# Retention in front of two feed-forward layers: late tokens in 64-token steps of all heads and two batches

## The chip, the cores and the metric

The kernel runs on one core of a Trainium2 chip. The metric is the device time of one execution in microseconds (us). TensorE multiplies matrices (rows named PE; PEld is the loading of its stationary operand), VectorE is DVE, ScalarE is ACT, GpSimd is POOL, and SyncE (SP) issues most of the DMAs. TensorE writes into PSUM, eight banks of 512 float columns in each of 128 partitions.

## The reference

Three layers follow each other: a retention with a decay for each head, and two feed-forward layers over all 3072 tokens.

```python
# q, k, v: (batch 4, heads 8, tokens 768, 64)
for t in range(768):
    state = gamma * state + outer(k[t], v[t])    # per batch and head, 64 x 64
    y[t]  = scale * q[t] @ state                 # gamma = 1 - 2**(-5 - head)
x  = y as (3072 tokens, 512)
x  = ELU(x @ w_in) @ w_out                       # 512 -> 2048 -> 512
h  = x @ w_in2
out = (P(h) / Q(h)) @ w_out2                     # P cubic, Q quadratic in |h|
```

## The kernel before

**Two phases.** Phase 0 is the retention and the first feed-forward layer, phase 1 the second one. The tokens go in six tiles `j` of 512 columns (`x_t[j]`), the hidden layer in 16 slices `f` of 128. One iteration of the loop in phase 0 is a pair (j, f). Its order is written out by hand in `seq`: tile 0 with f 0 to 7 (iterations 0 to 7), all of tile 1 (8 to 23), tile 0 with f 8 to 15 (24 to 31), then tiles 2, 3, 4 and 5 (32 to 95).

**One iteration.** `g1(h, f, ...)` is 12 matmuls into one PSUM bank `h`: each operand is split into a high part and a rest, and three products are summed. ACT makes Relu (L580) and Exp (L581), DVE joins them (L585), ACT rounds the result to `gh` (L593), POOL makes the rest `gl` (L594; on DVE in iterations 0 to 23). `g2` of the iteration before (`pend`) is 12 matmuls into four accumulators: eight that need `gh`, then four that need `gl`. So h of an iteration has a whole g2 and the next g1 on TensorE to be turned into gh and gl. After the last slice of a tile, `evac` copies the accumulators and stores them. The weights of both layers come as 64-bit floats and are narrowed and split by ACT, DVE and POOL beside this (`narrow`, `split_w`; iterations 0 to 18, and with odd f in tiles 2 to 4).

**Retention.** Each batch is cut into six chunks of 128 tokens, 24 chunks in all, batch after batch. A visit (an item i) does four heads of one chunk, so there are 48. Items 0 to 7 stand ahead of the loop, 8 to 15 in iterations 0 to 7, 16 to 23 in iterations 24 to 31, 24 to 47 in the iterations with even f of tiles 2 to 4. In a visit `at_out(i)` multiplies the state by q (not in a batch's first chunk), the masked scores by v, and the keys by v for the new state (not in its last), and `at_in(i + 1)` makes the next visit's scores q k. All these are plain float matmuls of 64 x 64 quarters of TensorE, with 64 or 128 columns; the four quarters are given in turn. The trace counts two passes for each such matmul: a visit's 28 matmuls are 56 rows. DVE masks the scores (L255), ACT and DVE make the high part and the rest of the output in the x tile (L320, L321), and write the new state. The visit stands between g1 and g2 on TensorE.

From chunk 8 on (the four batches' later chunks), the diagonal half-blocks of scores are laid out so that the output and the state come in two sums, and ACT and DVE add them (L316, L317, L307, L309); POOL scales q and k by the decay (L213, L216). The first eight chunks (`NV = 8`) keep the state's decay on TensorE by a diagonal matrix (`diag`), have their keys and queries scaled on DVE (L213, L216, called by `scale_chunk`), and the state's matmuls use two of the four quarters only.

**PSUM.** Four banks are accumulators, two are `h` (`psh`), two the tile of the visits (`T_t`). **DMA.** `load_chunk` fetches a chunk's q, k, v in three transfers of 512, 512 and 256 KB; SP's queue issues them and the weights in program order.

Of the kernel before, what the change touches and what calls it, by code (L numbers as in the profile page):

```python
# [21 lines left out]
C = 128  # L22
NP = H // 2
# [27 lines left out]
def decay_tables():  # L51

    g = 1.0 - 2.0 ** (-5.0 - np.arange(H, dtype=np.float64))
    scale = 1.0 / np.sqrt(D)
    t = np.arange(C)
    lag = np.maximum(t[None, :] - t[:, None], 0)
    full = scale * g[:, None, None] ** lag * (t[None, :] >= t[:, None])
    mask = np.zeros((2, 128, 2, 2, 3 * D))
    for q in range(2):
        for e in range(2):  # L60
            m0, m1 = full[4 * q + e], full[4 * q + 2 + e]
            mask[0, :D, q, e] = np.concatenate([m0[:D], m0[D:, D:]], axis=1)
# [8 lines left out]
    gc = rows(g ** C)  # L71
    gq = rows(scale * g[:, None] ** (t[None, :] + 1.0))
    dg = (gc[:, :, None] * np.tile(np.eye(D), (2, 1))[:, None, :]).reshape(128, -1)
    tab = np.concatenate([mask[0].reshape(128, -1), own_half(gk[None, :, :, None]).reshape(128, -1), gq, dg,
                          mask[1].reshape(128, -1), turned_halves(gk, 0), gc], axis=1)
    return np.ascontiguousarray(tab, dtype=np.float32)


@with_exitstack
def retention_ffn_kernel(ctx: ExitStack, tc: tile.TileContext, qkv, w1i, w1o, w2i, w2o, a_, b_, tab, out):  # L80
# [3 lines left out]
    CB = S // C  # L84
# [14 lines left out]
    atw = at.enter_context(tc.tile_pool(name="atw", bufs=2))  # L99
    psh = at.enter_context(tc.tile_pool(name="psh", bufs=2, space=PSUM))  # L100
    pst = at.enter_context(tc.tile_pool(name="pst", bufs=1, space=PSUM))
    NI = NCH * 2
# [61 lines left out]
    tab_t = acon.tile([128, 1292], F32, name="tab_t")  # L164
    gq_t = tab_t[:, 0:512].rearrange("p (g e t) -> p g e t", g=2, e=2)
    mk = [None, tab_t[:, 512:1288]]
    gc_t = tab_t[:, 1288:1292].rearrange("p (g e) -> p g e", g=2)
    St = acon.tile([128, 2, 2, D], F32, name="St")
    su = acon.tile([128, 2, D], F32, name="su")
# [17 lines left out]
    def of(c):  # L187
        qk, vk, q1 = pieces(c % 4 if c < 8 else c % 2)
# [4 lines left out]

    def load_qk(c):
        nc.sync.dma_start(out=pieces(c % 4 if c < 8 else c % 2)[0], in_=qkv[c, :, 0:1024])

    def load_rest(c):
        qk, vk, q1 = pieces(c % 4 if c < 8 else c % 2)
# [10 lines left out]

    def scale_chunk(c):  # L210
# [7 lines left out]
    A_t = {}  # L218
# [13 lines left out]
    def at_in(i):  # L232

        if i >= NI:
            return
        c, g = divmod(i, 2)
        q2, k2 = of(c)[0:2]
        T = T_t[i]
        if c < NV:
            for n in range(2):  # L240
                for p, e in ((0, 0), (0, 1), (1, 0), (1, 1)):
                    mm(T[R[p], e, 128 * n:128 + 64 * n], k2[R[e], 2 * g + p, D * n:D * n + D],
                       q2[R[e], 2 * g + p, D * n:C])
            return
        for p, e in ((0, 0), (0, 1), (1, 0), (1, 1)):
            mm(T[R[p], e, 64 * p:64 * p + 128], k2[R[e], 2 * g + p, 0:D], q2[R[e], 2 * g + p, :])
        for p, e in ((0, 0), (0, 1), (1, 0), (1, 1)):
            mm(T[R[1 - p], e, 128 * p:128 * p + D], k2[R[e], 2 * g + p, D:C], q2[R[e], 2 * g + p, D:C])

    def at_mask(i):  # L250
        if i >= NI:
            return
        A = atw.tile([128, 2, 192], F32, tag="A", name="A")
        A_t[i] = A
        nc.vector.tensor_tensor(out=A, in0=T_t[i][:, :, 0:192], in1=mk[i >= 2 * NV][:, 384 * (i % 2):384 * (i % 2) + 384]  # L255
                                .rearrange("p (e t) -> p e t", e=2), op=ALU.mult)

    def at_out(i):
# [3 lines left out]
        A, T = A_t.pop(i), T_t[i]  # L262
        four = ((0, 0), (1, 0), (0, 1), (1, 1))
        if c % CB:
            for p, e in four:
                mm(T[R[e], p, 192:320], St[R[p], g, e, :], q1[R[p], g, e, :], stop=False)
        if c < NV:
            at = lambda x, p, e, n: x[R[p], 4 * g + 2 * e + n, :]
            for n in range(2):
                for p, e in four:  # L270
                    mm(T[R[e], p, 192 + D * n:320], at(v, p, e, n), A[R[p], e, 128 * n:128 + 64 * n],
                       start=c % CB == 0 and n == 0, stop=n == 1)
            if c % CB != CB - 1:
                for e in range(2):
                    if c % CB:
                        for p in range(2):
                            mm(T[R[p], p, 384 + D * e:448 + D * e], diag[R[p], g, e, :], St[R[p], g, e, :], stop=False)
                    for n in range(2):
                        for p in range(2):
                            mm(T[R[p], p, 384 + D * e:448 + D * e], at(kn, p, e, n), at(v, p, e, n),  # L280
                               start=c % CB == 0 and n == 0, stop=n == 1)
            return
        for p, e in four:
            mm(T[R[e], p, 192:320], v[R[p], 4 * g + 2 * p + e, :], A[R[p], e, 64 * p:64 * p + 128], start=c % CB == 0)
        for p, e in four:
            mm(T[R[e], 1 - p, 320:384], v[R[1 - p], 4 * g + 2 * p + e, :], A[R[1 - p], e, 128 * p:128 * p + D])
        if c % CB != CB - 1:
            for e in range(2):
                for r, p in four:
                    h = 4 * g + 2 * p + e  # L290
                    mm(T[R[p], r, 384 + D * e:384 + D * e + D], kn[R[r], h, :], v[R[r], h, :])

    def at_state(i):
        c, g = divmod(i, 2)
        T, S = T_t[i], St[:, g]
        a, b = (T[:, r, 384:512].rearrange("p (e d) -> p e d", e=2) for r in range(2))
        if c % CB == CB - 1:
            return
        if c < NV:
            for p in range(2):  # L300
                nc.scalar.copy(S[R[p]], T[R[p], p, 384:512].rearrange("p (e d) -> p e d", e=2))  # L301
            return
        if c % CB == 0:
            nc.vector.tensor_copy(S, a)
        else:
            for e in range(2):
                nc.vector.scalar_tensor_tensor(out=S[:, e], in0=S[:, e], scalar=gc_t[:, g, e:e + 1], in1=a[:, e],  # L307
                                               op0=ALU.mult, op1=ALU.add)
        nc.vector.tensor_tensor(out=S, in0=S, in1=b, op=ALU.add)  # L309

    def at_x(i):
        c, g = divmod(i, 2)
        T = T_t[i]
        if c >= NV:
            for p in range(2):
                nc.scalar.copy(su[:, p], T[:, 1 - p, 320:384])  # L316
            nc.vector.tensor_tensor(out=T[:, :, 256:320], in0=T[:, :, 256:320], in1=su, op=ALU.add)  # L317
        o = T[:, :, 192:320]
        xs = [x[:, 2 * g:2 * g + 2, c % 4 * C:c % 4 * C + C] for x in x_tile(c // 4)]
        nc.scalar.copy(xs[0], o)  # L320
        return lambda: nc.vector.tensor_tensor(out=xs[1], in0=o, in1=xs[0].bitcast(F32), op=ALU.subtract)  # L321

# [14 lines left out]
    def g2(ph, j, f, gh, gl):  # L337
# [3 lines left out]
        if first:  # L341
            acc[ph, j] = [psa.tile([128, 512], F32, tag=f"acc{m}", name=f"acc{m}") for m in range(4)]
        ps = acc[ph, j]
        if ph == 1 and j == NB - 1 and f == KF - 1:
            for m in range(4):
# [3 lines left out]
                t0 = j * 512 + m * 128  # L349
# [10 lines left out]
        for lo in range(2):  # L360
# [7 lines left out]
        if last:  # L368
# [10 lines left out]
    def evac(ph, j, f):  # L379
        ps = acc.pop((ph, j))  # L380
        sign = -1.0 if ph else 1.0
        for a in range(2):
# [17 lines left out]
            else:  # L400
                t0 = j * 512 + a * 256
# [28 lines left out]
    mk[0] = t0[:, 0:776]  # L430
    diag = late("i13")[:, 0:256].rearrange("p (g e d) -> p g e d", g=2, e=2)
    load_qk(0)
    nc.scalar.dma_start(out=mk[0], in_=tab[:, 0:776])
# [3 lines left out]
    nc.scalar.dma_start(out=tab_t[:, 0:512], in_=tab[:, 776:1288])  # L437
    nc.scalar.dma_start(out=diag.rearrange("p g e d -> p (g e d)"), in_=tab[:, 1288:1544])
# [61 lines left out]
    for i in range(UP + 1, NI):  # L500
        T_t[i] = tiles[0]
# [240 lines left out]
```

## Time and profile before

| | |
|---|---|
| median of three runs | 1147.39 us (1147.37 to 1148.6) |
| the profiled execution | 1147.05 us, its span 1144.9 us |
| TensorE busy | 1127.5 us, 98% of the span |
| VectorE, ScalarE, GpSimd busy | 738.6, 702.5, 373.9 us |
| chain that ended last | TensorE 95% of the span |
| HBM | 79.84 MB read, 22.02 MB written |

The span is the stretch between the first and the last instruction in the profile; 2.15 us of the profiled execution lie outside it. Busy TensorE isn't TensorE at its peak, but where its work follows without a gap, its rows give the price of each piece of work.

### The profile page before, as it was taken

The numbers are of one execution on the slowest core, as the hardware profiler recorded it, in microseconds if no ns is written. First come the engines' busy times: TensorE is split into PE (matmuls) and PEld (weight loads), VectorE is DVE, ScalarE is ACT, GpSimd is POOL, SyncE is SP. The second block draws the span as 40 slices with busy tenths as digits, with TensorE's granted clock in tenths as the row PEclk, the third lists the DMA queues.
The fourth block names the chain that finished last, engine by engine and source line by source line (L and its number), as shares of the span: only waits on it lengthen the run. The fifth ranks groups of instructions, "written<-read, shape, count | busy, mean of one in ns | idle before, by whom it ended". The sixth has DMA issues, their size and how long they took to land.

```text
span 1144.9 us, 18306 instructions
## 1 busy us (share of the span) xinstructions
PE 1127.5 (98%) x7196; PEld 926.7 (81%) x7196; DVE 738.6 (65%) x1133; ACT 702.5 (61%) x1246; POOL 373.9 (33%) x289
## 2 busy tenths in 40 slices
PE   7799999999999999999999999999999999999998
PEld 6578888788888888888888888888888888888887
DVE  4887733354454454444353988888887888887875
ACT  3788733344444444445677877777767776776765
POOL 0334212333232243223786323322332232232222
PEclk9999999999999999999999999999999999999999
DMA  8666303263324434313554000200200200200000
GB/s 314 230 220 226 119 13 102 75 212 126 105 77 162 138 105 170 107 56 120 195 190 139 20 1 1 74 1 1 74 1 1 73 1 1 74 1 1 37 1 37
DMA packets 38229, 103.03 MB, mean 90 GB/s; under 512 B 4352, under 2 KB 4480, under 8 KB 38144
## 3 DMA queue, kind: packets, MB, share of 16 engines
q1 hardware_dynamic: 37280, 100.82, 26.4%
q8 instruction: 56, 0.92, 0.3%
q10 hardware_dynamic: 864, 1.06, 0.3%
q14 instruction: 29, 0.24, 0.1%
HBM read 79.84 MB, written 22.02 MB: 89 GB/s over the span
## 4 chain that ended last, share of the span: by engine, by line
PE 95%; ACT 1%; DVE 1%; POOL 1%; DMA 1%; issue 0%; SPq 0%; DVEq 0%; ACTq 0%; POOLq 0%
PE acc L325 46%; PE h L325 45%; PE r L230 5%; DMA ch<-in_qkv_dram 1%; DMA st<-in_w1o_dram 0%; POOL ch L216 0%; DVE A L255 0%; POOL gl L594 0%; POOL ch L213 0%; DVE ch L213 0%; ACT st L134 0%; ACT St L301 0%; ACT wc L132 0%; ACT xh L320 0%; POOL wo L160 0%
## 5 line engine op out<-in xcount | busy, mean ns | idle before, releaser
L325 PE MATMUL h<-xh,wi 128*128 128x512 f32 x1536 | 504.8, 390 | 4.2 <-POOL wi L160 3.0
L325 PEld LDWEIGHTS h<-xh,wi 128*128 128x128 f32 x1536 | 287.9, 188 | 66.9 <-POOL wi L160 5.6
L325 PE MATMUL h<-xl,wi 128*128 128x512 f32 x768 | 298.9, 389 | 0.0
L670 POOL TENSOR_TENSOR gl<-e,gh 128x512 fp32r<-128x512 f32 x96 | 124.8, 1300 | 349.5 <-ACT gh L669 213.3
L325 PE MATMUL acc<-gh,wo 128*128 128x512 f32 x768 | 195.2, 396 | 0.0
L325 PE MATMUL acc<-wo,gh 128*128 128x512 f32 x768 | 190.1, 389 | 0.0
L594 POOL TENSOR_TENSOR gl<-t,gh 128x512 fp32r<-128x512 f32 x72 | 94.1, 1307 | 293.2 <-ACT gh L593 191.8
L585 DVE SCALAR_TENSOR_TENSOR t<-t,h 128x512 f32<-128x512 f32 x72 | 49.5, 687 | 200.2 <-ACT t L581 200.2
L325 PEld LDWEIGHTS acc<-wo,gh 128*128 128x128 f32 x768 | 144.1, 188 | 29.9
L325 PEld LDWEIGHTS h<-xl,wi 128*128 128x128 f32 x768 | 144.1, 188 | 29.9
L325 PEld LDWEIGHTS acc<-gh,wo 128*128 128x128 f32 x768 | 141.1, 188 | 30.7
L580 ACT ACTIVATE t<-h 128x512 f32<-128x512 f32 x96 | 57.4, 598 | 159.4 <-PE h L325 145.2
L644 ACT ACTIVATE s<-h 128x512 f32<-128x512 f32 x96 | 57.4, 598 | 137.0 <-PE h L325 137.0
L650 DVE SCALAR_TENSOR_TENSOR u<-s,b,u 128x512 f32<-128x512 f32 x96 | 72.0, 750 | 55.8 <-ACT u L645 55.3
L325 PE MATMUL acc<-wo,gl 128*128 128x512 f32 x384 | 103.1, 389 | 0.0
L325 PE MATMUL acc<-gl,wo 128*128 128x512 f32 x384 | 102.9, 390 | 0.0
L660 DVE SCALAR_TENSOR_TENSOR e<-e,ab,r 128x512 f32<-128x512 f32 x96 | 72.2, 752 | 32.1 <-ACT r L654 32.1
L661 DVE SCALAR_TENSOR_TENSOR u<-u,r 128x512 f32<-128x512 f32 x96 | 87.7, 914 | 0.0
L325 PEld LDWEIGHTS acc<-gl,wo 128*128 128x128 f32 x384 | 72.1, 188 | 15.5
L325 PEld LDWEIGHTS acc<-wo,gl 128*128 128x128 f32 x384 | 72.0, 188 | 14.9
L646 ACT ACTIVATE e<-h,ab 128x512 f32<-128x512 f32 x96 | 75.4, 785 | 0.0
L653 DVE SCALAR_TENSOR_TENSOR e<-e,ab,h 128x512 f32<-128x512 f32 x96 | 71.8, 748 | 3.4
(83 smaller groups left out, 1338.4 us busy)
## 6 DMA issues: line engine op xcount, KB each, us to landing
ch<-in_qkv_dram SPq DMA_DIRECT2D x36, 512.0 KB, 4.8
st<-in_w1i_dram SPq DMA_DIRECT2D x16, 512.0 KB, 3.7
st<-in_w1o_dram SPq DMA_DIRECT2D x16, 512.0 KB, 4.6
st<-in_w2i_dram SPq DMA_DIRECT2D x16, 512.0 KB, 3.8
st<-in_w2o_dram SPq DMA_DIRECT2D x16, 512.0 KB, 4.6
wc<-w2s SPq DMA_DIRECT2D x32, 256.0 KB, 2.9
w2s<-wc SPq DMA_DIRECT2D x24, 256.0 KB, 2.2
xs<-y SPq DMA_DIRECT2D x24, 256.0 KB, 3.9
```

Of the source, the lines that this page charges most:

```text
L230: nc.tensor.matmul(out=out, lhsT=lhsT, rhs=rhs, start=start, stop=stop)
L325: nc.tensor.matmul(out=ps, lhsT=lh, rhs=rh, start=first and idx == 0, stop=last and idx == len(pairs) - 1)
L580: nc.scalar.activation(out=t, in_=h, func=ACTF.Relu, scale=-1.0)
L585: nc.vector.scalar_tensor_tensor(out=y, in0=t, scalar=-1.0, in1=h, op0=ALU.add, op1=ALU.max)
L594: (nc.vector if early else nc.gpsimd).tensor_tensor(out=gl, in0=y, in1=gh.bitcast(F32), op=ALU.subtract)
L644: nc.scalar.activation(out=s, in_=ps, func=ACTF.Square)
L646: nc.scalar.activation(out=e, in_=ps, func=ACTF.Identity, scale=ab[:, 3:4], bias=ab[:, 2:3])
L650: nc.vector.scalar_tensor_tensor(out=u, in0=s, scalar=b1, in1=u, op0=ALU.mult, op1=ALU.add)
L653: nc.vector.scalar_tensor_tensor(out=e, in0=e, scalar=ab[:, 1:2], in1=ps, op0=ALU.add, op1=ALU.mult)
L660: nc.vector.scalar_tensor_tensor(out=e, in0=e, scalar=ab[:, 0:1], in1=r, op0=ALU.add, op1=ALU.mult)
L661: nc.vector.scalar_tensor_tensor(out=u, in0=u, scalar=QC, in1=r, op0=ALU.add, op1=ALU.mult)
L670: nc.gpsimd.tensor_tensor(out=gl, in0=e, in1=gh.bitcast(F32), op=ALU.subtract)
```

## The change

The first eight chunks are now tokens 0 to 511 of batches 0 and 1, taken in turn (chunk c is batch c % 2), so the first two have no state before them, and all eight hand one on. All later tokens go in 64-token steps. A step takes all eight heads of two batches at once, in two halves s (one batch each). There are 16: steps 8 to 11 are the rest of batches 0 and 1 (iterations 25, 27, 29, 31), steps 12 to 23 batches 2 and 3 (f 1, 5, 9, 13 of tiles 2 to 4). Step 11 and 23 hand no state on, step 12 has none before it. In a step TensorE does g2 of the iteration before, then for each half the output and the state (`st_out`) and the next step's scores (`st_in`), then the eight gh matmuls of its own g2; the four gl matmuls follow the next iteration's g1. The output is scaled by decay on DVE after the matmuls (`st_y`) instead of q before them; ACT makes the decayed state (`st_decay`) for DVE to add (`st_sum`); POOL scales the keys alone, an iteration later. After iteration 23 the two h banks and the visits' tile become two tiles `V_t` of two banks: h of odd f is a bank of `V_t[1]`, of even f of `V_t[0]`, and the steps use columns of all four. Each x tile now holds 256 tokens of two batches, and `row` finds their place in the output.

```diff
+L = 64
...
-    CB = S // C
+    CB = S // L
...
     def load_rest(c):
-        qk, vk, q1 = pieces(c % 4 if c < 8 else c % 2)
-        if c % CB == CB - 1:
-            nc.sync.dma_start(out=vk[:, 0:512], in_=qkv[c, :, 1024:1536])
-        else:
-            nc.sync.dma_start(out=vk, in_=qkv[c, :, 1024:2048])
-        if c % CB:
+        qk, vk, q1 = pieces(c % 4)
+        nc.sync.dma_start(out=vk, in_=qkv[c, :, 1024:2048])
+        if c >= 2:
             nc.sync.dma_start(out=q1, in_=qkv[c, :, 2048:2560])
+    def load_step(n):
+        qk, vk, vq = pieces(n % 2)
+        nc.sync.dma_start(out=qk, in_=qkv[n, :, 0:1024])
...
     def scale_chunk(c):
         q2, k2, v, kn, q1 = of(c)
-        if c % CB:
-            (nc.vector if c < NV else nc.gpsimd).tensor_tensor(out=q1, in0=q1, in1=gq_t, op=ALU.mult)
-        if c % CB != CB - 1:
-            gk = mk[c >= NV][:, 768:776]
-            (nc.vector if 2 <= c < NV else nc.gpsimd).tensor_tensor(out=kn, in0=kn, in1=gk.to_broadcast([128, H, D]), op=ALU.mult)
+        if c >= 2:
+            nc.vector.tensor_tensor(out=q1, in0=q1, in1=gq_t, op=ALU.mult)
+        gk = mk[:, 768:776]
+        (nc.vector if c >= 2 else nc.gpsimd).tensor_tensor(out=kn, in0=kn, in1=gk.to_broadcast([128, H, D]), op=ALU.mult)
+
+    def scale_keys(n):
+        if n < NCH and n % CB != CB - 1:
+            kn = of_step(n)[3].rearrange("p b z s t -> p (b z) (s t)")
+            nc.gpsimd.tensor_tensor(out=kn, in0=kn, in1=gk_t.to_broadcast([128, 4, 2 * D]), op=ALU.mult)
...
+    four = ((0, 0), (1, 1), (0, 1), (1, 0))
+    def st_in(n, s):
+        if n >= NCH:
+            return
+        q2, k2 = of_step(n)[0:2]
+        T = U_t[n][s]
+        for z in range(2):
+            for a, r in four:
+                mm(T[R[r], a, z, 0:64], k2[R[a], r, z, s, :], q2[R[a], r, z, s, :])
+    def st_mask(n, s):
...
+        nc.vector.tensor_tensor(out=A, in0=U_t[n][s][:, :, :, 0:64], in1=mk_t, op=ALU.mult)
+    def st_out(n, s):
...
+        for z in range(2):
+            if n % CB:
+                for r, a in four:
+                    mm(T[R[a], r, 128 + 64 * z:192 + 64 * z], St[R[r], a, z, s, :],
+                       q2[R[r], r, z, s, :] if a == r else qf[R[r], z, s, :], stop=False)
+            for r, a in four:
+                mm(T[R[a], r, 128 + 64 * z:192 + 64 * z], v1[R[r], a, z, s, :], A[R[r], a, z, :], start=n % CB == 0)
+        if n % CB == CB - 1:
+            return
+        for z in range(2):
+            for a, r in four:
+                mm(T[R[r], a, 256 + 64 * z:320 + 64 * z], kn[R[a], r, z, s, :],
+                   v1[R[a], r, z, s, :] if a == r else v2[R[a], z, s, :])
+    def st_y(s):
...
+        nc.vector.tensor_tensor(out=y, in0=o, in1=gs_t, op=ALU.mult)
+    def st_sum(n, s):
...
+            nc.vector.tensor_tensor(out=S, in0=u, in1=G, op=ALU.add)
+    def st_decay(n):
+        if n % CB >= CB - 2:
+            return
+        for a in range(2):
+            for z in range(2):
+                nc.scalar.activation(out=Sg[:, a, z], in_=St[:, a, z], func=ACTF.Identity,
+                                     scale=gc_t[:, 2 * a + z:2 * a + z + 1])
+    def st_x(n):
...
+        nc.scalar.copy(xs[0], y)
+        nc.gpsimd.tensor_tensor(out=xs[1], in0=y, in1=xs[0].bitcast(F32), op=ALU.subtract)
...
-        visit = j == 0 and (f < HALF0 or f >= KF - 8) or (1 < j < NB - 1 and f % 2 == 0)
-        h = psh.tile([128, 512], F32, tag="h", name="h")
+        early = it < HALF0 + KF
+        visit = it < HALF0
+        step = not early and (j == 0 and f % 2 == 1 or 1 < j < NB - 1 and f % 4 == 1)
...
+        h = psh.tile([128, 512], F32, tag="h", name="h") if early else V_t[f % 2][:, f % 2]
         g1(h, f, xh, xl)
+        if half is not None and half[1] < KF - 1:
+            g2(0, *half, (1,))
+        half = None
...
+        if step:
+            g2(0, *pend)
+            pend = None
+            for s in range(2):
+                st_out(i, s)
+                st_in(i + 1, s)
+            for s in range(2):
+                st_y(s)
+                st_sum(i, s)
+                st_mask(i + 1, s)
+            st_x(i)
+            st_decay(i)
+            nx[0] += 1
+            half = (j, f, gh, gl)
+            g2(0, *half, (0, 1) if f == KF - 1 else (0,))
+            if i + 2 < NCH:
+                load_step(i + 2)
+            after = True
...
-        if (j, f) == (0, KF - 1):
+        if (j, f) == (0, KF - 2):
             load_ya()
...
-        pend = (j, f, gh, gl)
+        if not step:
+            pend = (j, f, gh, gl)
```

## Rows read from the trace of the kernel before

**Rows 1.** The page: busy time of the engines, the chain by line.

```profile
PE 1127.5 (98%) x7196; PEld 926.7 (81%) x7196; DVE 738.6 (65%) x1133; ACT 702.5 (61%) x1246; POOL 373.9 (33%) x289
...
PE acc L325 46%; PE h L325 45%; PE r L230 5%; DMA ch<-in_qkv_dram 1%; DMA st<-in_w1o_dram 0%; POOL ch L216 0%; DVE A L255 0%; POOL gl L594 0%; POOL ch L213 0%; DVE ch L213 0%; ACT st L134 0%; ACT St L301 0%; ACT wc L132 0%; ACT xh L320 0%; POOL wo L160 0%
```

**Rows 2.** The chain in time (start, length, what): an iteration without visit.

```profile
161.49 2.72 PE h L325 x12
164.21 2.72 PE acc L325 x12
```

**Rows 3.** The same chain: iteration 24, visits of four kinds, iteration 80's start.

```profile
177.81 2.72 PE h L325 x12
180.53 1.28 PE r L230 x56
181.81 2.97 PE acc L325 x12
...
223.07 1.05 PE r L230 x40
...
248.69 1.06 PE r L230 x48
...
520.22 0.71 PE r L230 x24
...
529.32 2.72 PE h L325 x12
```

**Rows 4.** Timeline around the visit of iteration 27: ACT and DVE turn h.

```profile
201.83 0.60 ACT L580 ACTIVATE t<-h 128x512 f32<-128x512 f32 x1 [3.13 <-PE h L325]
...
203.20 0.69 DVE L585 SCALAR_TENSOR_TENSOR t<-t,h 128x512 f32<-128x512 f32 x1 [3.85 <-ACT t L581]
```

**Rows 5.** Groups of instructions by shape: busy us, mean ns of one.

```profile
L594 POOL TENSOR_TENSOR gl<-t,gh 128x512 fp32r<-128x512 f32 x72 | 94.1, 1307 | 293.2 <-ACT gh L593 191.8 <-PE acc L325 101.3
...
L593 ACT CAST gh<-t 128x512 fp32r<-128x512 f32 x72 | 44.9, 623 | 34.2 <-DVE t L585 34.2
...
L321 DVE TENSOR_TENSOR xl<-r,xh 128x256 fp32r<-128x256 f32 x48 | 20.2, 421 | 10.0 <-ACT St L301 6.5 <-ACT xh L320 3.5
```

**Rows 6.** Busy time in stretches: PE, PEld, DVE, ACT, POOL, clock, DMA, GB/s.

```profile
13.00:18.00 5.00, 4.75 (x128) 4.62 (x120) 1.07 (x3) 1.32 (x5) 0.00 (x0) 0.66 1.03 411
48.00:92.00 44.00, 43.94 (x453) 34.68 (x453) 36.66 (x65) 37.62 (x72) 16.79 (x14) 1.00 0.70 234
240.00:336.00 96.00, 96.00 (x795) 78.42 (x797) 48.00 (x87) 43.13 (x85) 32.25 (x24) 1.00 0.39 129
```

**Rows 7.** Timeline of the start: chunk 2's load, items 2, 4 and 5.

```profile
5.71 0.45 SPq L195 DMA_DIRECT2D lo<-in_qkv_dram  x1
...
12.01 0.68 DVE L213 TENSOR_TENSOR ch<-ch,tab_t 128x512 f32<-128x512 f32 x1
...
12.74 0.55 PE L230 MATMUL r<-ch,St 64*64 64x128 f32 x8 [1.61 <-DVE ch L213]
...
14.85 0.48 PE L230 MATMUL r<-lo 64*64 64x128 f32 x2
...
17.82 0.56 DVE L255 TENSOR_TENSOR A<-r,li 128x384 f32<-128x384 f32 x1 [1.02 <-PE r L230]
```

**Rows 8.** DMA issues up to 40 us: count, size, us to landing.

```profile
lo<-in_qkv_dram SPq DMA_DIRECT2D x3, 512.0 KB, 9.0
```

**Rows 9.** The chain in time: visits of chunks 5, 6 and 7.

```profile
57.41 1.05 PE r L230 x40
...
64.47 1.29 PE r L230 x44
...
78.59 1.75 PE r L230 x60
```

**Rows 10.** Who waits for whom, whole span: total us, times, longest.

```profile
PE h L325 <- POOL wi L160: 3.0, 3, 1.5
```

**Rows 11.** The page: DMA issues of the retention's inputs.

```profile
ch<-in_qkv_dram SPq DMA_DIRECT2D x36, 512.0 KB, 4.8
```

More of the change, by code (lines that the diff above doesn't have):

```diff
@@ L261, in at_out @@
         q2, k2, v, kn, q1 = of(c)
-        A, T = A_t.pop(i), T_t[i]
+        A, T, S = of_a(i), T_t[i], St[:, :, g, c % 2]
         four = ((0, 0), (1, 0), (0, 1), (1, 1))
-        if c % CB:
+        if c >= 2:
             for p, e in four:
-                mm(T[R[e], p, 192:320], St[R[p], g, e, :], q1[R[p], g, e, :], stop=False)
-        if c < NV:
-            at = lambda x, p, e, n: x[R[p], 4 * g + 2 * e + n, :]
-            for n in range(2):
[L270 to L291, printed above, removed]
+                mm(T[R[e], p, 192:320], S[R[p], e, :], q1[R[p], g, e, :], stop=False)
@@ new lines, in at_out @@
+        at = lambda x, p, e, n: x[R[p], 4 * g + 2 * e + n, :]
+        for n in range(2):
+            for p, e in four:
+                mm(T[R[e], p, 192 + D * n:320], at(v, p, e, n), A[R[p], e, 128 * n:128 + 64 * n],
+                   start=c < 2 and n == 0, stop=n == 1)
+        for e in range(2):
+            if c >= 2:
+                for p in range(2):
+                    mm(T[R[p], p, 384 + D * e:448 + D * e], diag[R[p], g, e, :], S[R[p], e, :], stop=False)
+            for n in range(2):
+                for p in range(2):
+                    mm(T[R[p], p, 384 + D * e:448 + D * e], at(kn, p, e, n), at(v, p, e, n),
+                       start=c < 2 and n == 0, stop=n == 1)
@@ L293, in at_state @@
     def at_state(i):
         c, g = divmod(i, 2)
[L295 to L308, printed above, removed]
@@ L309, in at_state @@
-        nc.vector.tensor_tensor(out=S, in0=S, in1=b, op=ALU.add)
+        for p in range(2):
+            nc.scalar.copy(St[R[p], :, g, c % 2], T_t[i][R[p], p, 384:512].rearrange("p (e d) -> p e d", e=2))
     def at_x(i):
         c, g = divmod(i, 2)
[L313 to L318, printed above, removed]
@@ L359, in g2 @@
             return
-        for lo in range(2):
+        for lo in parts:
             for m in range(4):
@@ L367, in g2 @@
                 gemm3(ps[m], pairs, first and lo == 0, last and lo == 1)
-        if last:
+        if last and 1 in parts:
             evac(ph, j, f)
@@ L563, in fill @@
             load_next()
-    pend = None
+    pend = half = None
+    after = False
     for it, (j, f) in enumerate(seq):
@@ L586, in retention_ffn_kernel @@
         if visit:
-            at_mask(i + 1)
+            if i + 1 < 2 * NV:
+                at_mask(i + 1)
+            else:
+                for s in range(2):
+                    st_mask(NV, s)
             low = at_x(i)
@@ L596, in retention_ffn_kernel @@
             nx[0] += 1
-            if g == 1 and 8 <= c + 2 < NCH:
-                load_chunk(c + 2)
-            if g == 0 and c + 1 < 8 or g == 1 and 8 <= c + 1 < NCH:
+            if g == 1 and 8 <= c + 2:
+                load_step(c + 2)
+            if g == 0 and c + 1 < 8:
                 scale_chunk(c + 1)
+            if i + 1 == 2 * NV:
+                nx[0] = NV
+                st_decay(NV - 1)
+                after = True
+        elif after:
+            scale_keys(nx[0])
+            after = False
+        if step:
+            g2(0, *pend)
+            pend = None
+            for s in range(2):
+                st_out(i, s)
+                st_in(i + 1, s)
+            for s in range(2):
+                st_y(s)
[8 more added lines that the diff above has]
+                load_step(i + 2)
+            after = True
         if it == HALF0:
```

182 lines of the change are left out of this document (118 added, 64 removed).

## Prediction, written before the changed kernel was run

> **What bounds the kernel now.** First the page: TensorE is busy 98% of the span, and the chain that ended last goes through its g1, g2 and retention matmuls for 96% [rows 1]. So a saving elsewhere is worth nothing unless TensorE waits for it, and a matmul removed is worth what it holds TensorE. Next the chain in order of time, where pieces of TensorE's work stand end to end. An iteration without visit is g1 2.72 and g2 2.72, 5.44 us [rows 2]. A full visit takes 1.28 for its 56 passes, and the g2 behind it 2.97 instead of 2.72 [rows 3]: 1.53 us. From the start of iteration 24 (177.81) to that of iteration 80 (529.32) are 351.51 us [rows 3]; 56 iterations without visits would be 304.64. The 32 late visits with all their waits thus cost 46.9 us. That is what the steps replace. Last the stretches: in the late one (240 to 336 us) TensorE is busy all the time, DVE and ACT half of it, POOL a third; from 48 to 92 us DVE and ACT are busy 36.7 and 37.6 of 44 us [rows 6]. So the late part has room beside TensorE, the early loop little.
>
> **Price of a 64-column pass.** The four kinds of visit differ by whole blocks. A first chunk lacks the state's four matmuls (eight passes of 128 columns): 56 rows become 48 and 1.28 becomes 1.06, so 27.5 ns for each. A last chunk lacks eight matmuls of 64 columns that use all four quarters (16 passes): 1.05, so 14.4 ns [rows 3]. Of the 56 passes 24 are wide and 32 narrow: 0.66 + 0.46, which leaves 0.16 us for the entry. The last visit of all has 16 wide and 8 narrow: 0.16 + 0.44 + 0.12 = 0.72, and its row says 0.71 [rows 3]. The price holds.
>
> The page TensorEngine Tiling (Array Packing) of the Trainium skill, section Instruction Overhead, speaks against the change: it gives each matmul some 60 cycles of overhead and advises against tiling by a dimension that is already small. If that stood on top of 64 columns as of 128, a narrow pass would cost two thirds of a wide one, an estimate of 18 ns from that page, and the sum below would be 7 us higher. Here it is 14.4 ns against 27.5, so no such overhead shows [rows 3].
>
> **The late part, step by step.** Each full step has for each half 8 matmuls with the state, 8 with the scores, 8 for the state, 8 new scores, all of 64 columns: 64 in all, 128 passes. Step 11 (no state out) and step 12 (none in) have 48, step 23 (no state out, no next scores) 32. The 16 steps have 13 x 64 + 48 + 48 + 32 = 960 matmuls, 1920 passes, 27.6 us at 14.4 ns. Every step is entered and left once: 0.16 and 0.25, 16 x 0.41 = 6.6. Sum 34.2 against 46.9: **12.7 us less**. All four quarters have the same share in each group of four, as in the late visits, so I take their price; half of a wide pass (13.75) would be 1.3 us better, and 17 ns, a guess toward the mean of a whole visit (1.28 / 56 = 22.9), 5.0 worse.
>
> **Does TensorE wait in a step?** I count from the end of g1(f). Relu, Exp and join take the time from 201.83 to 203.89 [rows 4], 2.1 us; gh comes 0.65 later, gl 1.3 after it [rows 5]. TensorE does g2 of f-1 until 2.72, half 0 until about 3.8, half 1 until 4.8, its own eight gh matmuls (1.81, two thirds of a g2) until 6.6. Half 1 overwrites h of f, free at 2.1 where it is wanted at 3.8. gh is there at 2.75, wanted at 4.8; gl at 4.1, wanted after the next g1 at 9.3. The next g1 overwrites columns that `st_y`, `st_sum` and `st_mask` of half 0 read: three DVE operations on 256 columns, 0.42 each by the nearest row [rows 5], from 3.4 to 4.7, wanted at 6.6. Ahead of them on DVE stand two `narrow` operations of the odd f, which run during g1. So each wait has 1.5 us or more of slack, and I cost it at nothing; without the cover of the eight gh matmuls the g1 would have 0.1 us left. Behind a step no g2 is pending, so gh of f+1 has 0.91 + 2.72 = 3.6 us instead of 5.4, and needs 2.8. The DVE work of a step (some 2.5 us) and ACT's (output rounding 0.62, four decays) replaces that of two visits, on engines half idle [rows 6]. POOL loses a query scaling for each chunk and gains 1.3 us of output rest.
>
> One place is tighter: step 11 is in iteration 31, and the g1 of iteration 32 reads the x tile that it completes. From half 1's end this takes `st_y` 0.42, rounding 0.62, the rest on POOL 1.31 and hops, 2.5 to 2.8 us; the whole own g2 (2.72) stands before it. I take 0.3, bounds 0 to 1.
>
> `load_step` issues three transfers after a step for the step after next; SP waits there for half 1 alone. They land in 4.8 us [rows 11], with 13 us to spare even in the two-iteration steps of tile 0. Nothing.
>
> **The early part.** Chunk 1 has no state, so its queries are neither loaded nor scaled. TensorE waited 1.61 us at item 2 for that scaling on DVE [rows 7]; it is late next for chunk 2's q and k, issued at 5.71 [rows 7] and landing 9.0 later [rows 8], at 14.7, just where the row at 14.85 stands. The 256 KB not loaded bring that forward by 0.6 at 411 GB/s [rows 6]. Item 3 also lacks four wide and four narrow matmuls, 0.45. So item 5's mask (17.82 now) comes about **1.1 us earlier**, and the chain behind it. But chunk 5 now hands its state on: its keys are scaled on DVE in iteration 0, 0.68 us like the query scaling [rows 7], in a stretch where TensorE waits for freshly split weights [rows 10]: **0.7 more**. In iterations 2 and 3 chunk 5's visits grow from 1.05 to the 1.75 of a full early one, in 4 and 5 chunk 6's from 1.29 to 1.75 (its row misses four records) [rows 9]: 1.4 + 0.9, of which I let 0.6 fall into waits there: **1.7 more**. Iteration 7 makes 32 narrow passes of scores instead of 16 mixed ones (0.46 against 0.34): 0.1. Together **+1.4**; bounds -1 (start gains as much as the 1.61 and more, DVE hides the rest) and +4 (no gain at the start, and ACT and DVE, 85% busy, stretch two iterations).
>
> **Sum.** 1147.05 - 12.7 + 1.4 + 0.3 = 1136.05. The profiled execution is 0.3 below the median, so I say **1136 us**.
>
> **Rivals.** *Passes cost the same at any width.* If TensorE's bound is its instructions, 1920 passes at 22.9 ns are 44.0, with 16 x 0.25 48.0: the late part loses 1.1 where I have it gain 12.7, and the time is 1150, slower. For it: the count of late passes doesn't fall (22 x 56 + 4 x 48 + 5 x 40 + 24 = 1648 before). Against: the two differences above, 27.5 and 14.4. It decides from 20 ns a pass on, where 1920 passes and the entries eat the 11 us of gain. The rule of the Trainium skill named above (TensorEngine Tiling (Array Packing), Instruction Overhead) would end between the two, near 1143 by its 60 cycles. *The step's banks.* h shares its banks with the steps. Should DVE be late (its queue also holds narrowing in just these iterations), each step would stop TensorE at the next g1 or at half 1. At 1 us a step, 16 us: 1152, slower; it turns the gain from 0.69 us a step. Against: 1.5 to 2 us of slack, DVE half idle. *The early loop is the price.* DVE and ACT limit iterations 0 to 7, and more work there stretches them: +4 instead of +1.4, 1139, still faster. For it: 85% busy [rows 6].
>
> **How the numbers follow.** My forecast 0.70 (1132 to 1140), passes whose price falls little with their width 0.07, banks 0.08, early loop 0.12, all else (late transfers, a wait that I don't see) 0.03. A measurement of this kernel tells 0.2% (2.3 us) from no change. Forecast and early loop are faster, 0.82, and small forms of the banks (under 0.5 us a step) add 0.04: faster 0.86. Within 0.2% 0.03, slower 0.11. The range: 1136 less 1.3 (half a wide pass), less 2.4 (early bound) and a little, 1131; upward 17 ns (5.0), early +2.6, part of the banks: 1145.
>
> **What would show it.** Right: 5.44 us iterations as before, steps of some 1.9 us for 128 passes plus 0.41, no TensorE wait for DVE at g1 behind a step, 339 us from iteration 24 to 80, item 5's mask near 16.7. Wrong: narrow passes in a long run above 17 ns; waits of h on DVE or ACT after steps; iterations 0 to 7 longer by 4 us than before.

## The result, and the profile after

The changed kernel takes 1138.07 us (median of four runs, 1136.88 to 1139.07) where the kernel before takes 1147.38 beside it; the ratio is 0.9916, interval 0.9899 to 0.9933. It is faster by 9.3 us. The prediction said 1136 and a range of 1131 to 1145. The late part came out as costed, to 0.3 us; the early part costs, in three profiles of this kernel, 0.4 to 3.1 us more than the 1.4 that it was given.

The profiled execution of the changed kernel took 1139.07 us, its span 1137.3. First the page: busy time of the engines, granted clock, chain by line.

```profile
PE 1119.1 (98%) x7532; PEld 924.9 (81%) x7532; DVE 714.6 (63%) x1056; ACT 707.5 (62%) x1222; POOL 378.0 (33%) x292
...
PEclk8999999999999999999999999999999999999999
...
PE acc L379 46%; PE h L379 28%; PE r L379 17%; PE r L256 4%; DMA lo<-in_qkv_dram 1%; ACT st L141 0%; ACT wc L139 0%; ACT t L657 0%; ACT t L656 0%; POOL wi L167 0%; DVE ch L236 0%; DVE A L270 0%; POOL wo L167 0%; ACT St L299 0%; DVE lo L236 0%
```

TensorE is the bound as before [rows 1]; from iteration 24 on, g1 writes a bank of `V_t`, so its rows are now called r L379, and all retention is r L256. The chain in order of time, from iteration 24:

```profile
182.29 2.72 PE r L379 x12
...
193.17 2.02 PE r L256 x128
195.19 2.04 PE acc L379 x8
197.24 2.72 PE r L379 x12
199.96 0.91 PE acc L379 x4
...
232.57 1.56 PE r L256 x96
...
509.42 1.09 PE r L256 x64
...
521.62 2.72 PE r L379 x12
```

Iteration 24 starts at 182.29 and iteration 80 at 521.62: 339.33 us, where the kernel before has 351.51 [rows 3] and the prediction 338.8 and 0.3 for a wait. A full step holds TensorE for its 128 passes 2.02, and the eight matmuls behind it take 2.04 instead of 1.81: 2.25, the predicted 128 x 14.4 ns + 0.41. From 128 to 64 passes the row falls by 0.93, 14.5 ns each. So the late part gained 12.2 us. But iteration 24 starts 4.5 us later than before (182.29 against 177.81 [rows 3]); from the start of iteration 80 to the end of the span it is 615.7 us, 615.6 before. So what this execution lost against the forecast lies ahead of iteration 24.

No matmul waits for DVE or ACT in a full step. The timeline of the step at 269 us shows why: half 0's three DVE operations end at 271.53, half 1 ends at 271.2, and the own gh matmuls then hold TensorE until the next g1 at 273.35.

```profile
270.44 0.42 DVE L350 TENSOR_TENSOR A<-r,tab_t 128x256 f32<-128x256 f32 x1 [1.73 <-PE r L256]
270.78 0.41 DVE L360 TENSOR_TENSOR St<-r,Sg 128x256 f32<-128x256 f32 x1
271.12 0.41 DVE L326 TENSOR_TENSOR A<-r,tab_t 128x256 f32<-128x256 f32 x1
```

One wait there is, beside the place where 0.3 us were set for it. The chain around iteration 33:

```profile
237.08 2.73 PE r L379 x12
...
241.98 0.63 ACT gh L672
...
242.65 3.02 PE acc L379 x12
```

Iteration 32's g1 follows without a gap, so the x tile was ready. But iteration 31 does its whole g2 in the step, so iteration 33's g1 alone hides the turning of iteration 32's h, and the g2 at 242.65 stands behind gh by about 0.1, and is slow by 0.3.

The start, by the timeline (item 4, the scores of the items behind it, item 6 on TensorE, with what it waited for), and item 6 in the chain:

```profile
17.26 0.45 PE L256 MATMUL r<-lo,St 64*64 64x128 f32 x8 [1.59 <-DVE lo L236]
...
22.54 0.81 PE L256 MATMUL r<-li 64*64 64x128 f32 x15 [2.11 <-issue]
...
24.93 0.71 PE L256 MATMUL r<-lo,St 64*64 64x128 f32 x8 [1.59 <-DVE lo L236]
...
24.93 2.64 PE r L256 x48
```

and by stretches (PE, PEld, DVE, ACT, POOL, granted clock, DMA, GB/s), the clock falling behind these idle times:

```profile
13.00:18.00 5.00, 3.09 (x94) 2.60 (x95) 2.98 (x6) 2.22 (x6) 0.00 (x0) 1.00 1.03 411
18.00:25.00 7.00, 3.30 (x112) 2.98 (x107) 3.44 (x8) 2.88 (x8) 0.00 (x0) 0.84 0.77 308
25.00:30.00 5.00, 5.00 (x112) 4.99 (x112) 2.94 (x6) 2.35 (x6) 0.87 (x1) 0.55 0.56 189
...
48.00:54.00 6.00, 4.82 (x41) 3.58 (x43) 4.91 (x10) 4.67 (x10) 1.12 (x1) 0.72 0.39 126
```

Item 5's mask starts at 15.72 instead of 17.82 [rows 7] (predicted 16.7), so 2.1 us were gained there; the clock from 13 to 18 us, 1.00 where it was 0.66 before [rows 6], has a part in it. Then TensorE stands 2.11 us, until 22.54, without waiting for another engine, and after it runs near half clock (1.2 GHz of 2.4) from 25 to 30 us: item 6 starts with the kernel before, and its 48 passes take 2.64.

This stand has a companion in the trace. The DMA queues from 20.1 to 20.3 us show one 16 KB packet of the instruction queue:

```profile
q8 instruction: 1, 0.02, 29.3%
```

It starts at 20.20, 2.34 us before the stand ends. The profiles of all runs have 14 such stands (0.16 us or more, from 8 us on, with no releaser), all between small matmuls, and each ends 2.26 to 2.48 us after a packet of this kind started. So TensorE probably stood for its own next instructions, and an earlier start then only brings a longer stand. No run moved these packets, so this is not shown by experiment.

At 49 us, after 1.76 us of waiting for iteration 2's weights, the clock falls once more. Last the early loop in the chain:

```profile
49.18 3.95 PE h L379 x10
53.13 1.90 PE r L256 x60
...
60.69 1.75 PE r L256 x60
...
90.42 1.88 PE r L256 x78
```

The visits of iterations 3 to 6 are 1.75 now, as predicted, where they were 1.05, 1.29 and 1.75 [rows 9]; iteration 2's takes 1.90 as the clock comes back, and iteration 7's 1.88 with the first step's scores.

### The profile page after: what moved, and what is told of

It reads as the page before. It is cut to its first block, busy times and chain, and to the rows that moved or that the text cites. A ratio compares the mean times of both kernels' runs of the same rounds, so it can differ in the third digit from the quotient of the medians.

```text
span 1137.3 us, 18835 instructions
## 1 busy us (share of the span) xinstructions
PE 1119.1 (98%) x7532; PEld 924.9 (81%) x7532; DVE 714.6 (63%) x1056; ACT 707.5 (62%) x1222; POOL 378.0 (33%) x292
## 4 chain that ended last, share of the span: by engine, by line
PE 96%; ACT 1%; DMA 1%; DVE 1%; issue 0%; POOL 0%; SPq 0%; ACTq 0%; DVEq 0%
PE acc L379 46%; PE h L379 28%; PE r L379 17%; PE r L256 4%; DMA lo<-in_qkv_dram 1%; ACT st L141 0%; ACT wc L139 0%; ACT t L657 0%; ACT t L656 0%; POOL wi L167 0%; DVE ch L236 0%; DVE A L270 0%; POOL wo L167 0%; ACT St L299 0%; DVE lo L236 0%
## 5 line engine op out<-in xcount | busy, mean ns | idle before, releaser
L379 PE MATMUL h<-xh,wi 128*128 128x512 f32 x960 | 316.5, 391 | 3.7 <-POOL wi L167 2.4
L379 PEld LDWEIGHTS h<-xh,wi 128*128 128x128 f32 x960 | 180.5, 188 | 42.9 <-POOL wi L167 3.6
L379 PE MATMUL acc<-gh,wo 128*128 128x512 f32 x768 | 193.0, 393 | 0.1
L379 PE MATMUL acc<-wo,gh 128*128 128x512 f32 x768 | 190.1, 389 | 0.0
L379 PE MATMUL r<-xh,wi 128*128 128x512 f32 x576 | 188.8, 389 | 0.0
L379 PE MATMUL h<-xl,wi 128*128 128x512 f32 x480 | 187.2, 390 | 0.0
L379 PEld LDWEIGHTS acc<-wo,gh 128*128 128x128 f32 x768 | 144.1, 188 | 29.9
L379 PEld LDWEIGHTS acc<-gh,wo 128*128 128x128 f32 x768 | 142.3, 188 | 30.9 <-ACT gh L672 0.6
L660 DVE SCALAR_TENSOR_TENSOR t<-t,r 128x512 f32<-128x512 f32 x72 | 49.3, 685 | 186.5 <-ACT t L657 186.5
L379 PEld LDWEIGHTS r<-xh,wi 128*128 128x128 f32 x576 | 108.1, 188 | 22.5
L379 PE MATMUL r<-xl,wi 128*128 128x512 f32 x288 | 112.0, 389 | 0.0
L656 ACT ACTIVATE t<-r 128x512 f32<-128x512 f32 x72 | 42.7, 593 | 101.0 <-PE r L379 101.0
L379 PEld LDWEIGHTS h<-xl,wi 128*128 128x128 f32 x480 | 90.4, 188 | 18.6
L379 PE MATMUL acc<-wo,gl 128*128 128x512 f32 x384 | 103.1, 389 | 0.0
L379 PE MATMUL acc<-gl,wo 128*128 128x512 f32 x384 | 102.6, 389 | 0.0
L672 ACT CAST gh<-t 128x512 fp32r<-128x512 f32 x72 | 44.7, 621 | 66.6 <-DVE t L660 66.6
```

Source lines behind the costliest of these rows:

```text
L379: nc.tensor.matmul(out=ps, lhsT=lh, rhs=rh, start=first and idx == 0, stop=last and idx == len(pairs) - 1)
L656: nc.scalar.activation(out=t, in_=h, func=ACTF.Relu, scale=-1.0)
L660: nc.vector.scalar_tensor_tensor(out=y, in0=t, scalar=-1.0, in1=h, op0=ALU.add, op1=ALU.max)
L672: nc.scalar.copy(gh, y)
```

## The experiments

Theory A: the late part's terms are right, and the early loss is the start's gain, given back by the stand of TensorE and a lower clock, with the keys' scaling of chunk 5. Theory B: it is the early loop's longer visits, with the DVE and ACT work beside them. This table has for each run the median, its ratio to the kernel before with the interval, where the chain has the start of iteration 24, the stretch from there to iteration 80, and the granted clock from 0 to 60 us in the profile. Differences between kernels under 2 us lie inside these intervals, so medians alone don't show them; they are told by medians beside the stretches in the profiles.

| run | us | ratio | iteration 24 | to 80 | clock |
|---|---|---|---|---|---|
| before | 1147.38 | 1 | 177.81 | 351.51 | 0.97 |
| changed | 1138.07 | 0.9916 (0.9899-0.9933) | 182.29 | 339.33 | 0.91 |
| c_after | 1137.63 | 0.9915 (0.9901-0.9928) | 181.02 | 339.34 | 0.94 |
| c_after2 | 1138.16 | 0.9916 (0.9902-0.9930) | 179.61 | 339.31 | 0.97 |
| e_batch | 1137.32 | 0.9912 (0.9898-0.9925) | 180.54 | 339.34 | 0.94 |
| e_q1 | 1137.47 | 0.9913 (0.9899-0.9926) | 180.29 | 339.34 | 0.97 |
| e_kn5pool | 1137.48 | 0.9912 (0.9899-0.9926) | 181.70 | 339.31 | 0.91 |
| e_scores2 | 1146.56 | 0.9991 (0.9981-1.0000) | 180.44 | 347.70 | 0.97 |
| e_apart | 1149.73 | 1.0013 (1.0004-1.0023) | 180.92 | 351.49 | 0.94 |
| e_whole | 1142.50 | 0.9956 (0.9941-0.9971) | 180.13 | 344.76 | 0.97 |
| e_light | 1136.73 | 0.9906 (0.9893-0.9920) | 180.26 | 339.31 | 0.94 |
| e_light2 | 1135.43 | 0.9891 (0.9877-0.9906) | 179.57 | 339.32 | 0.94 |
| e_four | 1138.09 | 0.9922 (0.9909-0.9936) | 181.36 | 339.31 | 0.89 |
| e_four2 | 1136.13 | 0.9896 (0.9879-0.9912) | 179.59 | 339.31 | 0.94 |

**c_after, c_after2: the changed kernel again.** No edit.

> The changed kernel once more, beside the others. 1138 us (1136.9 to 1139.1 so far). If the stand of TensorE at 20 us and the half clock behind it are what spreads its runs, this profile shows them again in some size; the stretch from iteration 24 to 80 is 339.3 us whatever the start does.

> The changed kernel once more, beside the next two: 1137.6, iteration 8 starting at 92.9 to 93.8 in the profile (95.1 in the first one, with 10 us of half clock in the start and iteration 2).

The stretch to iteration 80 is the same to 0.03 us. Iteration 24 starts 1.3 and 2.7 us sooner than in the first profile, with the clock: at 0.97, the clock of the kernel before, the early part is 1.8 us longer than before (179.61 against 177.81), at 0.91 it is 4.5. The stand at 20 us does not come again; c_after has 0.65 us of one until 15.7 us, and in both TensorE does item 4 at a lowered clock instead (0.50 and 0.53 from 18 to 20.4 us). c_after2's median is 1138.16, not 1137.6, and its iteration 8 starts at 92.4, sooner than expected. The early part falls into two pieces, by the first matmuls of iterations 2 and 8 in the timelines (in brackets the difference to before):

| profile (clock) | iteration 2 | from 2 to 8 | together |
|---|---|---|---|
| before (0.97) | 45.52 | 45.09 | |
| c_after2 (0.97) | 44.82 (-0.70) | 47.59 (+2.50) | +1.80 |
| c_after (0.94) | 45.33 (-0.19) | 48.49 (+3.40) | +3.21 |
| changed (0.91) | 46.68 (+1.16) | 48.41 (+3.32) | +4.48 |

Item 6 of c_after2 in the chain, and the wait for iteration 2's weights in its timeline and in the first profile's:

```profile
24.21 1.50 PE r L256 x48
```

```profile
47.32 0.73 PE L379 MATMUL h<-xh,wi 128*128 128x512 f32 x2 [1.76 <-POOL wi L167]
49.18 0.73 PE L379 MATMUL h<-xh,wi 128*128 128x512 f32 x2 [1.76 <-POOL wi L167]
```

So the 4.48 of the first profile are the 1.80 of c_after2, 1.86 at the start (item 6 comes 0.72 later and takes 1.14 longer at the lowered clock), and 0.82 in the loop, where the clock fell in iteration 2. The same 1.76 us of waiting is followed by that fall in the first profile and by none in c_after2 (1.00 from 48 to 54 us). Execution against execution at the clock of 0.97, the change is worth 10.7 us (1147.05 against 1136.37), where the prediction had 11.0 (12.7 less 1.4 and 0.3).

**e_scores2: the price of narrow passes.**

```diff
-        for z in range(2):
+        for z in (0, 1, 0, 1):
             for a, r in four:
                 mm(T[R[r], a, z, 0:64], k2[R[a], r, z, s, :], q2[R[a], r, z, s, :])
```

> Every step makes the next step's scores twice, into the same place: 16 x 32 = 512 more passes of 64 columns in a long run, nothing else. At the 14.4 ns of the prediction 7.4 us more, 1145.4. If passes cost the same at any width (22.9 ns) 11.7 more, 1149.8. By the 18 ns between, 9.3 more, 1147.3.

It takes 8.4 to 8.9 more than the changed kernel. The chain has a full step of 160 passes, and the waits of TensorE between 184 and 525 us one line:

```profile
271.14 2.49 PE r L256 x160
273.63 2.04 PE acc L379 x8
```

```profile
PE r L256 <- issue: 1.1, 1, 1.1
```

32 more passes are 0.47 us, 14.7 ns each, in the 15 steps of this stretch 7.05; 1.1 of the rest is one stand without a releaser, which ends 2.46 us after an instruction packet started. By the time alone, 8.4 to 8.9 lies between 14.4 ns (7.4) and 18 ns (9.3); the row decides. The terms of the sum hold in a run of 160 passes too, and the rival of passes that cost the same at any width is out, as is the price of 18 ns.

**e_apart: the price of entering.**

```diff
-            g2(0, *pend)
-            pend = None
             for s in range(2):
                 st_out(i, s)
                 st_in(i + 1, s)
+                if s == 0:
+                    g2(0, *pend)
+                    pend = None
```

> In each step the g2 of the iteration before stands between half 0 and half 1, so the small matmuls are entered and left twice. If each entry with the slower g2 behind it costs 0.41 us, 16 x 0.41 = 6.6 us more, 1144.6. If that price is one of the step (its waits) and not of the switch, no change: 1138.

It takes 11.6 to 12.1 more. A step in the chain, and TensorE's wait between 184 and 525 us:

```profile
273.10 1.09 PE r L256 x64
274.19 2.95 PE acc L379 x12
277.14 1.09 PE r L256 x64
278.23 2.04 PE acc L379 x8
```

```profile
PE r L256 <- POOL ch L243: 4.2, 3, 2.3
```

The four rows sum to 7.17, where the step with the g2 ahead has 2.72 + 2.02 + 2.04 = 6.78: 0.39 for one more entry, 6.2 in 16 steps, as expected. The other half was not foreseen: half 0 now comes one g2 earlier, and where a step stands only two iterations behind the one before it, POOL has not yet scaled its keys. In three such steps (iterations 27, 29 and 33) TensorE waits 4.2 us, and the clock falls after the last wait (0.79 from 246 to 254 us), where a g2 takes 4.49 instead of 2.95. In the changed kernel that g2 is the cover of the key scaling.

**e_whole: the cover of the split g2.**

```diff
-            half = (j, f, gh, gl)
-            g2(0, *half, (0, 1) if f == KF - 1 else (0,))
+            if f == KF - 1:
+                g2(0, j, f, gh, gl)
...
-        if not step:
+        if not (step and f == KF - 1):
             pend = (j, f, gh, gl)
```

> A step's own g2 isn't split: it follows the next iteration's g1 as it did before the change (but for iteration 31). The next g1 then stands right behind half 1, and by the count in the prediction DVE is done with half 0 just then; by the trace of the changed kernel 0.2 us later. So 0 to 0.25 us for each of 15 steps, 1138 to 1142, with TensorE waiting for DVE's masking at g1. If the split is without use, 1138 with no such wait; if h's bank is held longer than DVE's three operations, more than 1142.

It takes 4.3 to 4.9 more, a little over the upper end. The chain and the wait:

```profile
268.96 1.14 PE r L256 x64
...
270.88 0.34 DVE A L326
...
271.26 3.01 PE r L379 x12
```

```profile
PE r L379 <- DVE A L326: 4.3, 14, 0.5
```

The g1 behind the step waits for half 0's mask, 0.31 each time. The prediction's "0.1 us left" without this cover was 0.4 off (DVE starts later than counted), and the order of the split g2 is worth 4 to 5 us of the 9.3. This is the rival of the step's banks, made true: it costs 0.36 a step here, under the 0.69 that would turn the gain.

**e_batch, e_q1, e_kn5pool: three ways of undoing a part of the start.** Chunks batch after batch again; chunk 1's queries loaded and scaled for nothing; chunk 5's keys on POOL.

```diff
# e_batch (layout, state index and output rows follow)
-        if c >= 2:
+        if c % 4:
             nc.sync.dma_start(out=q1, in_=qkv[c, :, 2048:2560])
# e_q1 (the same in scale_chunk)
-        if c >= 2:
+        if c >= 1:
             nc.sync.dma_start(out=q1, in_=qkv[c, :, 2048:2560])
# e_kn5pool
-        (nc.vector if c >= 2 else nc.gpsimd).tensor_tensor(out=kn, ...)
+        (nc.vector if c >= 2 and c != 5 else nc.gpsimd).tensor_tensor(out=kn, ...)
```

> The first eight chunks go batch after batch again (four chunks of batch 0, then four of batch 1); the steps stay. The same matmuls as in the changed kernel, but chunk 1 has a state again and chunk 4 has none. Theory A, the gain at the start is lost to a stand of TensorE and the half clock behind it: the start runs as before the change, without that stand, the scaling of chunk 4's queries falls away ahead of iteration 0, iteration 2's visit comes near 50 us instead of 53, and the time is 1135 to 1136, 2 to 3 less than the changed kernel. Theory B, the early loop's longer visits and its ACT and DVE work are the whole loss: the same as the changed kernel within 0.7, 1138.

> Chunk 1's queries are loaded and scaled again, though nothing reads them: 256 KB more in the queue and 0.68 us more on DVE, as before the change. Theory A: what TensorE starts later at chunk 2 it no longer stands at 20 us, so the time is the same, 1137.5 to 1138.5, and the stand is shorter than 2.1 us. Theory B, the start's gain counts: 0.7 to 1.3 slower, 1138.8 to 1139.4.

> Chunk 5's keys are scaled on POOL instead of DVE, in iteration 0. If the 0.7 us that I gave this scaling on DVE are right, the weights of iteration 2 come earlier and the time is 0.4 to 0.7 less than the changed kernel, 1137.4. If DVE had room there, or POOL's work slows DVE beside it, no change: 1138, or up to 0.5 more.

By medians all three take what the changed kernel takes beside them (1137.3 to 1137.5, c_after 1137.6). The timeline of e_batch, then e_q1's stand and its first matmul of iteration 2:

```profile
19.20 0.45 PE L256 MATMUL r<-lo,St 64*64 64x128 f32 x8 [1.63 <-DVE lo L236]
24.87 0.45 PE L256 MATMUL r<-lo,St 64*64 64x128 f32 x8 [2.04 <-DVE lo L236]
```

```profile
22.68 0.56 PE L256 MATMUL r<-li 64*64 64x128 f32 x15 [1.42 <-issue]
...
45.50 0.47 PE L379 MATMUL h<-xh,wi 128*128 128x512 f32 x1
```

In e_batch item 4 starts at 19.20, two microseconds after the changed kernel's 17.26, and item 6 at 24.87 with it. Its 1135 to 1136 did not come: it has no stand, but its clock falls all the same, later (0.89 from 30 to 48 us, 0.76 from 48 to 54). In e_q1 the stand is 1.42 us, shorter as expected. Its median gives the start's gain up at no price, as theory A said, but a median can't tell 0.7 us here. Its profile can be set beside c_after2's: the clock is 0.97 in both, and from iteration 2 to 8 both take 47.59 us, while iteration 2 starts 0.68 later (45.50 against 44.82) and iteration 24 too (180.29 against 179.61). In this pair the start's gain counts, 0.7 us, as theory B said. That is a hint and no proof: the falls of the clock stand in different places in the two, and item 6, at 24.84 in e_q1, starts at 24.21, 24.70 and 24.93 in the three profiles of the changed kernel. So whether the start's gain counts is open between the theories; the stand and the clock move as much as it is worth. Chunk 5's keys on DVE show no cost by themselves, but a cost under 1 us would not show in these medians.

**e_light, e_light2: the early loop's added work left out.**

```diff
# e_light
+        if c == 5:
+            return                    # ahead of the new state's matmuls and of its copies
...
-            if c >= 2:
+            if c >= 2 and c != 6:     # at both uses of the state
# e_light2, in scale_chunk besides
-        if c >= 2:
+        if c >= 2 and c != 6:
             nc.vector.tensor_tensor(out=q1, in0=q1, in1=gq_t, op=ALU.mult)
+        if c == 5:
+            return
```

> Leaves out of the early loop what the order by turns adds to it: chunk 5 hands no state on (its matmuls for the state and their copies are left out) and chunk 6 uses none, as chunks 5 and 6 had it before the change; the scaling of keys and queries stays. If the longer visits in iterations 2 to 5 are what is lost early, iteration 8 starts at 90.4 to 90.8 as before the change, and the time is 2.2 to 2.6 less than the changed kernel, 1135.2. If the scaling on DVE or the start is the loss, less than 1 is given back.

> As e_light (chunk 5 hands no state on, chunk 6 uses none), and chunk 5's keys and chunk 6's queries aren't scaled either, so that DVE has the work of before the change in iterations 0 to 7. If the early loss is the visits' matmuls and this DVE work together, in a loop whose weights come from DMA, ACT, DVE and POOL just in time, the stretch from iteration 2 to 8 is 45.1 to 45.6 us as before the change (46.6 in e_light, 47.6 in the changed kernel), and the time is 1 to 1.5 less than e_light, 1135.5. If the state's copies and matmuls alone were the loss, 46.6 again and 1136.7.

Both leave out work that the result needs. By medians e_light gives back 0.9 to 1.4 instead of 2.2 to 2.6, and its iteration 8 starts at 93.2, not at 90.4 to 90.8; e_light2 gives back 2.2 to 2.7, 1135.43 where 1135.5 was expected. The chain of e_light around its iteration 3:

```profile
57.06 2.58 PE h L383 x10
59.65 1.05 PE r L256 x40
```

The visit is back at 1.05, but g1 has stopped after two of its matmuls until 57.06, for weights that POOL has just split. By the timelines' first matmuls, iterations 2 to 7 take 45.1 us before, 47.6 in c_after2 and 46.6 in e_light. e_light2's profile does not show the 45.1 to 45.6 that I expected: it has 47.5, with a lowered clock around 48 us (ten matmuls of g1 take 4.12) and a wait for a weight's DMA. So its median speaks for theory B's loop, but its interval still touches that of the changed kernel, and its one profile does not settle how much lies in iterations 2 to 7.

**e_four, e_four2: can the early loop be shorter?** The new state on all four quarters; then also two copies on DVE and later keys on POOL.

```diff
+        both = ((0, 0), (1, 0), (0, 1), (1, 1))
+        to = lambda p, e: T[R[p ^ e], p, 384 + D * e:448 + D * e]
...
+        for n in range(2):
+            for p, e in both:
+                mm(to(p, e), at(kn, p, e, n), at(v, p, e, n), start=c < 2 and n == 0, stop=n == 1)
...
# e_four2
-                nc.scalar.copy(St[R[p], e, g, c % 2], T_t[i][R[p ^ e], p, 384 + D * e:448 + D * e])
+                (nc.scalar.copy if e == 0 else nc.vector.tensor_copy)(St[R[p], e, g, c % 2], ...)
-        (nc.vector if c >= 2 else nc.gpsimd).tensor_tensor(out=kn, ...)
+        (nc.vector if 2 <= c < 4 else nc.gpsimd).tensor_tensor(out=kn, ...)
```

> The early visits make the new state with all four quarters of TensorE instead of two (the second head of each pair writes the other half of the partitions), and ACT copies the state in four pieces instead of two. A full early visit has 24 such passes, at 29 ns now and 14.6 then: 0.35 us less for each of the eight visits in the loop, where TensorE is the bound, 2.0 to 2.8 less, 1135.3. If ACT is the bound there (four copies take 0.3 longer than two), no change or up to 2 more.

> As e_four, with less on ACT and DVE: two of the four state copies on DVE, and the keys of chunks 4 to 7 scaled on POOL. If ACT and DVE were what took e_four's gain, the stretch from iteration 2 to 8 is 46 us or less and the time 1136; if the weights' DMAs or POOL bind next, 47 to 48 and 1137 to 1138.

The chain of e_four:

```profile
53.03 5.49 DMA st<-in_w1o_dram
...
64.33 2.56 PE h L380 x10
66.89 1.40 PE r L256 x64
```

A visit's 64 passes take 1.40 instead of 1.75, just the 0.35 expected, and the time is the same: the chain now goes through a weight's DMA, ACT and POOL, and g1 waits; its profile also has the lowest clock of all, 0.89. With ACT and DVE relieved, e_four2 takes iterations 2 to 7 in 45.8 us and 1136.13 in all, as expected. It is the fastest of the kernels that do the whole work, 1.5 to 2.0 us under the changed one by medians (the intervals overlap) and 1.04% under the kernel before.

## Why the prediction was right, and where it was off

- *Price of a narrow pass, 14.4 ns*: right; 14.5 from the steps' rows, 14.7 from e_scores2. It took 1648 passes of before to 1920 and still gained, since 728 wide ones (27.5 ns) went.
- *Entry and exit, 0.41*: right; 0.39 by e_apart. Half of the late gain is this alone: 32 x 0.41 less 16 x 0.41 is 6.6 of 12.2.
- *No wait in a step*: right for the order as it is, with less slack than counted where the split g2 covers (e_whole). The pending g2 as the cover of the key scaling, where steps are two iterations apart, was not named in the prediction; without it three steps wait 4.2 us (e_apart).
- *0.3 us at iteration 32*: the size was right, the place not: the x tile is in time, gh of iteration 32 is not.
- *Late part*: 12.7 less and 0.3 back; measured 12.2 less.
- *Early part, +1.4*: the term that was mis-sized. It measured +1.8, +3.2 and +4.5 in the three profiles of the changed kernel; the parts were:
  - *The loop, +2.5* (0.7 for keys, 1.7 for visits, 0.1): measured +2.50 where the clock did not fall in it, 3.3 to 3.4 where it did. That the sum fits so well is partly luck. The 0.7 does not show by itself (e_kn5pool), and the visits' rows alone grew by 2.45 (0.70, 0.70, 0.46, 0.46 and 0.13), of which the prediction let 0.6 fall into waits. How matmuls and DVE work share the 2.5 isn't shown: taking the matmuls away gives back 0.9 to 1.4 (e_light), the scaling as well 2.2 to 2.7 (e_light2), shorter matmuls alone nothing (e_four).
  - *The start, -1.1*: measured -0.7, -0.2 and +1.2. The step that failed is "the chain behind it": item 5's mask did come 1.5 to 2.1 us earlier, but TensorE then ran at a lowered clock or stood until 22.5 us, and item 6 came only 0.1 to 0.9 earlier.
  - *The clock* was not costed at all. It and the stand are the 2.7 us between the best and the worst of these profiles.
- *The number*: 1136 is met by the execution whose early clock is that of the kernel before (c_after2's profile, 1136.37). The median, 1138.07, is 2.1 over it, and most executions have the lower clock: by the mean clock on record for each, two of twelve have 0.998 (1136.4 and 1136.9), the others 0.995 to 0.997 (1137.4 to 1139.1). At 0.997 the kernel before takes 1147.9 on average (19 executions), the changed one 1137.9 (5). The rival of the early loop, 1139, came nearer to the median than 1136, but not by its mechanism: where the clock held, the loop stretched by the 2.5 that was costed.
- *What is open*: what the start's gain is worth (e_q1), whether the instruction packets make the stand, and why the clock falls in some executions and not in others behind the same wait. No experiment tried the last two by themselves.

## What to carry to other kernels

Cost a stretch where one engine is always busy by differences of its own rows, by shape and by entry: four kinds of visit gave two prices and an overhead that held to 0.2 us over 340. Where several engines are 85% busy and feed each other just in time, a shorter matmul alone gave nothing here (e_four), and the added visits cost about what their matmuls take; there, and where the clock moves from run to run, a sum of single costs should be given a wide bound on the bad side. When two variants differ by less than their executions scatter, a median that stays the same is no proof that an edit has no price (e_q1); look in the profiles for where the clock fell. And ask of each instruction that stands between a producer and its use what it covers: moving one g2 uncovered a key scaling, splitting another hid a mask.

## What the runs showed of the hardware

Four plain float matmuls on the four 64 x 64 quarters run side by side: a pass of 64 columns costs 14.4 to 14.7 ns, in runs of 64 to 160 passes alike, about half of a pass of 128 (27.5), and twice that where two quarters alone are used (e_four's 0.35 us for 24 passes). Going from full-size matmuls to quarters and back costs 0.39 us (e_apart). In dense runs of small matmuls TensorE can stand, for up to 2.34 us (e_light), without waiting for another engine: 14 such stands in 11 of the 14 profiles, each ending 2.26 to 2.48 us after a 16 KB packet of the instruction queue started; that the packet is the cause is likely, not shown. The granted clock of the first 60 us differs between executions of one program (0.91, 0.94 and 0.97 in three profiles of the changed kernel), the two falls of the first one behind the waits at 22.5 and 49.2 us shown above, and iteration 24 starts 182.3, 181.0 and 179.6 us in. A wait of 1.76 us came with a fall of the clock once and without one once, at the same place of the program.
